# Wider tiles and a re-dealt queue: x in pairs of chunks, N=512 projections, one gate pass and 8 KB weight slots

## The chip, the cores and the metric

One core of a Trainium2 chip runs the kernel. The metric is device time in microseconds (us), the median of several executions; lower is better. A "span" is the time from the first to the last instruction in one profiled execution; here the time is 1.7 to 1.9 us longer than the span. Engines: PE is the matmul engine (PEld its weight loads), DVE the vector engine, ACT the scalar engine, POOL and SP issue transfers. The program fixes the order of each engine's queue, and an entry waits for those ahead of it (in e9 below, the silu, moved behind a scan, starts on DVE at 202.91 instead of 193.59 us).

A run is called slow here only when it lies over 1.5% above the fastest run of the same kernel; where that matters the text says so.

## The reference, cut to what matters

```python
g = sigmoid((x * gate_w).sum(-1))                # gate per token; x is 2048 x 1024, bf16
# A: diagonal state-space layer over the 2048 tokens
Bu = x @ B_bar.T                                 # complex, 1024 states       ("S1")
h[t] = Lam_bar * h[t-1] + Bu[t]                  # recurrence over time       (scans)
a = 2 * Re(h @ C.T) + x * Dskip                  #                            ("S2")
# B: the 8 tokens with the largest x @ w_r go through an expert
idx = argsort(-(x @ w_r))[:8];  xs = x[idx]
y = (silu(xs @ w_gate) * (xs @ w_up)) @ w_down   # weights 1024 x 3584, and 3584 x 1024
b = x + scatter(idx, y * sigmoid(r[idx]))
out = g * a + (1 - g) * b
```

## The kernel before

Time is cut into 8 chunks of 256 tokens. For each chunk PE computes S1, ACT evicts it into V, DVE rotates V (three products, `dve_m`, called "m"), scans it (`dve_scan`) and rotates back (`dve_post`) into H, and PE computes S2 from H. PE also runs the gate pass, the selection of 8 tokens ("sel_a" to "sel_d", with DVE steps in between) and the expert: gate and up products, silu on DVE (`silu_b`), 7 transposes of it (`silu_t`), and the down product `y`.

The order on each engine is fixed by hand: `at(position, f)` queues `f` after the PE work at that position, and entries that fall due together go out in order of their number.

```python
# S1, 256 columns per matmul; [cut]
for dc in range(KD):
    nc.tensor.matmul(vps[:, pl, c, :], lhsT=BT[pl][:, dc, ct * P:(ct + 1) * P], rhs=xT[k][:, dc, :], start=(dc == 0), stop=(dc == KD - 1))
nc.scalar.copy(out=V[k][:, :, 2 * cp:2 * cp + 2, :], in_=vp.pop((k, cp))[:])      # 1024 columns per eviction

# gate pass: x is the stationary side, 2 columns move; 128 matmuls in all; [cut]
nc.tensor.matmul(zc[:, j, :], lhsT=xT[k][:, dc, tl * P:(tl + 1) * P], rhs=rg[:, dc, :], ...)

# order, [cut]
at((2, 7.1), lambda: (dve_post(1, 0, 8), gq.pop("r")(), sel_a2()))      # ahead of m of chunk 2
at((3, 4.1), sel_b2)                                                    # ahead of the scan of chunk 2
at((6, 6.1), silu_a)
at((6, 6.3), silu_b)
# ... the scan of chunk 6 stands at (6, 6.5): behind silu_b
at((7, 1.5), silu_t)
d_pos = [(7, 4)] * 7 + [(8, 4)] * 7                                     # down weights, 512 KB each, freed one by one
```

## Time and profile before

| | before |
|---|---|
| time | 252.34 us (252.07 to 253.46, 4 runs) |
| span | 250.8 us |
| PE / DVE / ACT busy | 244.3 / 232.9 / 101.6 us |
| mean granted clock of PE | 0.999 |

From the page of the kernel before: busy time of each engine; PE's busy share and its granted clock, both in tenths, in 40 slices of the span; the chain that ended last, by engine; and the two large matmul groups (count, then busy us and mean ns of one, then idle time ahead of them).

```profile
PE 244.3 (97%) x1986; PEld 164.2 (65%) x1986; DVE 232.9 (93%) x230; ACT 101.6 (41%) x143; POOL 41.3 (16%) x58
...
PE   8799999999999999999999999999999999999994
...
PEclk9999999999999999999999999999999999999999
...
PE 49%; DVE 41%; SPq 3%; DMA 3%; issue 2%; ACT 0%; DVEq 0%
...
L253 PE MATMUL vps<-xT,BT 128*128 128x256 bf16 x1024 | 114.2, 273 | 1.6 <-DMA BT<-in_A_B_re_dram 0.8
...
L716 PE MATMUL zps<-CT,H 128*128 128x512 bf16 x480 | 105.8, 379 | 0.0
```

The mean of 273 and 379 ns is latency, since matmuls overlap. The pace is read from the chain of waits (start, us, what), where consecutive matmuls are merged:

```profile
15.59 24.63 PE vps L253 x224
...
55.39 10.36 PE zps L716 x48
```

24.63 us for 224 matmuls is 110 ns each at 256 columns; 10.36 us for 48 is 216 ns each at 512. PE runs at that pace from 15.6 to 247.5 us without a gap over 0.5 us. DVE idles for 2.45 us at 84 us and is otherwise full until its last H at 240.9 us, when the last S2 tile has just begun. Both engines are full. From the time lines of PE and of DVE (start, us, engine, line, instruction, count):

```profile
187.42 7.15 PE L253 MATMUL vps<-xT,BT 128*128 128x256 bf16 x64
194.92 0.56 PE L662 MATMUL aT_ps<-ident,gr 128*128 128x128 bf16 x7 [0.35 <-DVE gr L657]
195.32 7.15 PE L253 MATMUL vps<-xT,BT 128*128 128x256 bf16 x64
```

```profile
193.59 0.62 DVE L656 TENSOR_TENSOR sl_e<-gr,sl_e 128x896 bf16<-128x896 bf16 x1
194.24 0.62 DVE L657 TENSOR_TENSOR gr<-sl_e,gr 128x896 bf16<-128x896 bf16 x1
194.78 8.73 DVE L288 TENSOR_TENSOR_SCAN U<-d,U 128x2048 bf16<-128x2048 f32 x2
```

The silu (`gr`) comes just ahead of a 8.7 us pair of scans, and PE waits 0.35 us for it.

### The profile page before, as it was taken

What the parts mean: (1) busy time and instruction counts of PE and PEld (TensorE: products, weight loads), DVE (VectorE), ACT (ScalarE), POOL (GpSimd) and SP (SyncE); (2) the same over time, 40 slices, a digit from 0 to 9 for tenths busy, and PEclk for the clock granted to TensorE, in tenths of its full rate; (3) what the DMA queues carried; (4) which work ended last, traced back from release to release, by engine and by line L of the source; (5) the groups of instructions that cost most, each with busy time, mean ns of one, the idle gap of its engine ahead of it and who ended that gap; (6) DMA issues with size and microseconds to landing.
All of it is one profiled execution on the core that took longest, in us unless ns stands there. A gap on an engine that the chain in (4) does not pass through costs nothing.

```text
span 250.8 us, 4677 instructions
## 1 busy us (share of the span) xinstructions
PE 244.3 (97%) x1986; PEld 164.2 (65%) x1986; DVE 232.9 (93%) x230; ACT 101.6 (41%) x143; POOL 41.3 (16%) x58
## 2 busy tenths in 40 slices
PE   8799999999999999999999999999999999999994
PEld 5688889884678447874487644876448864454453
DVE  1899999999999599999999999999999999999992
ACT  3679981535212322535121372131732335264411
POOL 4020000000000067201400240013101400141520
PEclk9999999999999999999999999999999999999999
DMA  7999999999900202819795587869999829966072
GB/s 182 228 158 238 179 258 211 251 260 261 312 0 3 73 0 89 167 31 348 156 358 190 203 232 236 277 216 338 262 288 293 183 46 277 302 169 178 3 167 84
DMA packets 63492, 48.31 MB, mean 193 GB/s; under 512 B 49504, under 2 KB 51168, under 8 KB 63472
## 3 DMA queue, kind: packets, MB, share of 16 engines
q1 hardware_dynamic: 59056, 37.23, 56.6%
q0 software_dynamic: 4224, 10.53, 17.5%
q8 instruction: 15, 0.25, 0.4%
q10 hardware_dynamic: 192, 0.27, 0.3%
q14 instruction: 5, 0.04, 0.1%
HBM read 27.55 MB, written 8.40 MB: 143 GB/s over the span
## 4 chain that ended last, share of the span: by engine, by line
PE 49%; DVE 41%; SPq 3%; DMA 3%; issue 2%; ACT 0%; DVEq 0%
PE vps L253 22%; PE zps L716 21%; DVE U L288 14%; DVE U L277 4%; DVE U L279 4%; DVE V L278 4%; DVE U L313 4%; DVE H L315 4%; DVE H L311 4%; DVE xt L691 3%; PE zl L730 3%; DMA xT<-in_A_x_dram 3%; SPq L89 2%; PE y L647 1%; PE zc L468 1%
## 5 line engine op out<-in xcount | busy, mean ns | idle before, releaser
L253 PE MATMUL vps<-xT,BT 128*128 128x256 bf16 x1024 | 114.2, 273 | 1.6 <-DMA BT<-in_A_B_re_dram 0.8
L253 PEld LDWEIGHTS <-BT 128*128 128x128 bf16 x1024 | 99.4, 98 | 15.6 <-issue 1.8
L716 PE MATMUL zps<-CT,H 128*128 128x512 bf16 x480 | 105.8, 379 | 0.0
L716 PEld LDWEIGHTS <-H 128*128 128x128 bf16 x480 | 46.3, 98 | 55.7 <-issue 1.9
L288 DVE TENSOR_TENSOR_SCAN U<-d,U 128x2048 bf16<-128x2048 f32 (+1 forms) x20 | 61.7, 3128 | 0.4
L258 ACT CAST V<-vps 128x1024 bf16<-128x1024 f32 x32 | 32.3, 1009 | 60.9 <-PE vps L253 60.9
L719 ACT ACTIVATE ot<-zps,gcol 128x512 bf16<-128x512 f32 x30 | 20.6, 688 | 67.8 <-PE zps L716 65.0
L693 POOL DMA_DIRECT2D out_dram<-xt x14 | 7.8, 561 | 93.1 <-DVE xt L691 92.6
L687 ACT ACTIVATE e<-Dbc,omgcol,gcol 128x1024 f32<-128x1024 bf16 x16 | 18.9, 1233 | 0.0
L691 DVE TENSOR_TENSOR xt<-xt,e 128x1024 bf16<-128x1024 bf16 x16 | 18.8, 1218 | 0.0
L278 DVE TENSOR_TENSOR V<-V,nTi 128x4096 bf16<-128x4096 bf16 (+1 forms) x10 | 16.5, 1652 | 0.5
L277 DVE TENSOR_TENSOR U<-V,T2tab 128x4096 bf16<-128x4096 bf16 (+1 forms) x10 | 16.5, 1645 | 0.5
L279 DVE TENSOR_TENSOR U<-U,V 128x4096 bf16<-128x4096 bf16 (+1 forms) x10 | 16.5, 1652 | 0.3
L554 POOL DMA_INDIRECT xsel<-in_A_x_dram,idx_c x1 | 6.4, 6387 | 61.3 <-ACT ot L719 61.3
L313 DVE TENSOR_TENSOR U<-U,S2tab 128x4096 bf16<-128x4096 bf16 (+1 forms) x8 | 16.2, 2025 | 0.3
L315 DVE TENSOR_TENSOR H<-H,U 128x4096 bf16<-128x4096 bf16 (+1 forms) x8 | 16.2, 2025 | 0.3
L311 DVE TENSOR_TENSOR H<-U,Ctab 128x4096 bf16<-128x4096 bf16 (+1 forms) x8 | 16.1, 2018 | 0.0
L740 POOL DMA_DIRECT2D out_dram<-ot x14 | 14.3, 1048 | 2.0 <-DMA out_dram<-yc,idx_c 2.0
L682 POOL DMA_DIRECT2D xt<-in_A_x_dram x12 | 8.2, 684 | 13.6 <-DMA out_dram<-xt 13.6
L346 DVE TENSOR_TENSOR_SCAN U<-D,U 128x1024 bf16<-128x1024 f32 x4 | 8.9, 2278 | 0.0
L635 PE MATMUL pgu<-wgu,xsel 128*32 128x448 bf16 x128 | 7.4, 355 | 0.0
L730 PE MATMUL zl<-CT,H 128*128 128x256 bf16 (+1 forms) x48 | 7.1, 308 | 0.0
(145 smaller groups left out, 127.9 us busy)
## 6 DMA issues: line engine op xcount, KB each, us to landing
wgu<-in_B_w_gate_dram SPq DMA_DIRECT2D x16, 448.0 KB, 6.4
wgu<-in_B_w_up_dram SPq DMA_DIRECT2D x16, 448.0 KB, 5.7
wd<-in_B_w_down_dram SPq DMA_DIRECT2D x12, 512.0 KB, 6.7
out_dram<-xt POOLq DMA_DIRECT2D x14, 256.0 KB, 2.8
...
```

The lines of the kernel that those rows point to most:

```text
L253: nc.tensor.matmul(vps[:, pl, c, :], lhsT=BT[pl][:, dc, ct * P:(ct + 1) * P], rhs=xT[k][:, dc, :], start=(dc == 0), stop=(dc == KD - 1))
L258: nc.scalar.copy(out=V[k][:, :, 2 * cp:2 * cp + 2, :], in_=vp.pop((k, cp))[:])
L277: nc.vector.tensor_tensor(out=u, in0=v, in1=T2tab[:, :, c0:c1, :], op=ALU.mult)
L278: nc.vector.tensor_tensor(out=v, in0=v, in1=bc(nTi, c0, c1), op=ALU.mult)
L279: nc.vector.tensor_tensor(out=u, in0=u, in1=V[k][:, ::-1, c0:c1, :], op=ALU.add)
L288: nc.vector.tensor_tensor_scan(out=fl, data0=d0[:, c0:c1, :].rearrange("p c t -> p (c t)"), data1=fl, initial=0.0, op0=ALU.mult, op1=ALU.add)
L311: nc.vector.tensor_tensor(out=h, in0=g, in1=bc(Ctab, c0, c1), op=ALU.mult)
L313: nc.vector.tensor_tensor(out=g, in0=g, in1=S2tab[:, :, c0:c1, :], op=ALU.mult)
L315: nc.vector.tensor_tensor(out=h, in0=h, in1=G[k][:, ::-1, c0:c1, :], op=ALU.add)
L691: nc.vector.tensor_tensor(out=xt[:], in0=xt[:], in1=es.pop(b)[:], op=ALU.mult)
L716: nc.tensor.matmul(zps[:], lhsT=H[k][:, pl, ct, tl * P:(tl + 1) * P], rhs=CT[pl][:, ct, dsl], start=(ct == 0 and pl == 0), stop=(ct == NCT ...
L719: nc.scalar.activation(out=ots[b][:, dsl], in_=zps[:], func=ACT.Copy, scale=gcol[:, b:b + 1])
```

## The change

The intent is less PE time: an N=512 matmul reads each weight tile once for two chunks, and a column-tiled gate pass (four weight tiles of 32 columns side by side in PE's array) needs 32 matmuls in place of 128. Chunk x tiles become pairs (`X[m]`), so S1 alternates with S2 in larger blocks: S1 of chunks 2 and 3; S2 of 0 and 1; S1 of 4 and 5; S2 of 2 and 3; S1 of 6 and 7; S2 of 4 to 7. Expert weights are loaded two to a slot of 8 KB per partition, which the x pairs release. All of this needed a new order of queues.

```diff
+    def s1u(m, ct, pl, k0, k1):                       # one weight tile, 512 columns of two chunks
+        o = vp[m, ct][:, pl, k0:k1, :].rearrange("p k t -> p (k t)")
+        ... nc.tensor.matmul(o, lhsT=BT[pl][:, dc, ct * P:(ct + 1) * P], rhs=X[m][:, dc, k0 * LC:k1 * LC], ...)
+    def s1e(m, ct):                                   # two evictions of 512 columns, one for each chunk
+        ... nc.scalar.copy(out=V[k][:, :, ct, :], in_=vp[m, ct][:, :, kk, :])
-    ... zc[:, j, :], lhsT=xT[k][:, dc, tl * P:(tl + 1) * P], rhs=rg[:, dc, :]
+    ... zr[32 * m:32 * m + 32, :], lhsT=rg[:, dc, :], rhs=X[m][:, dc, :]        # 4 column tiles, then 4 transposes
+    def moe_slot(s):
+        for i in range(2):
+            moe_item(2 * s + i, wq[s][0][:, i])
+        free_w.append(wq.pop(s)[1])                   # a slot is released after both its weights are used
+        load_w()
[... cut ...]
+    at((1, 1.5), lambda: dve_m(2, 0, 8))
+    at((1, 1.6), sel_a2)                              # now behind m of chunk 2
+    at((1, 3.9), sel_b)
+    at((2, 1.5), lambda: dve_scan(2, 0, 8))
+    at((2, 2.0), sel_b2)                              # now behind the scan of chunk 2
[... cut ...]
+    at((7, 1.95), silu_a)
+    at((7, 1.96), silu_b)
+    at((7, 3.9), silu_t)
+    at((7, 0.5), lambda: dve_m(6, 0, 8))
+    at((7, 1.5), lambda: dve_scan(6, 0, 8))           # now ahead of silu_b
[... cut ...]
+    pos = [(3, 2.9)] * 2 + ... + [(7, 1.9)] * 2 + [(8, 0.9)] * 4 + [(8, 3.9)] * 3      # the last 7 slots are down weights
+    blocks = [(1, None), (None, 0), (None, 1), (2, None), (None, 2), (None, 3), (3, None)] + [(None, k) for k in range(4, NK)]
```

More of the change, by code (lines that the diff above doesn't have):

```diff
@@ L69, with load_B @@
     ps_m = ctx.enter_context(tc.tile_pool(name="ps_m", bufs=2, space=PSUM))
-    xT = [const.tile([P, KD, LC], BF16, name=f"xT{k}", tag=f"xT{k}") for k in range(5)]
+    X = {}
     BT = [const.tile([P, KD, NP_], BF16, name=f"BT{pl}") for pl in range(2)]
     CT = [const.tile([P, NCT, D], BF16, name=f"CT{pl}") for pl in range(2)]
-    x0r = const.tile([P, BPC, D], BF16, name="x0r", tag="xT5")
+    x0r = const.tile([P, BPC, D], BF16, name="x0r", tag="XP2")
     for tl in range(BPC):
         nc.sync.dma_start(x0r[:, tl, :], x2d[tl * P:(tl + 1) * P, :])
+    def load_B(pl, c0, c1):
+        nc.sync.dma_start_transpose(BT[pl][:, :, c0 * P:c1 * P], Bsrc[pl][c0 * P:c1 * P, :])
+    for pl in range(2):
+        load_B(pl, 0, 2)
     vrow = small.tile([NCT, 5, P], BF16, name="vrow", tag="va")
@@ L80, with new_X, load_X @@
         nc.scalar.dma_start(vrow[:, i, :], v.rearrange("(c p) -> c p", p=P))
+    def new_X(m):
+        X[m] = const.tile([P, KD, 2 * LC], BF16, name=f"X{m}", tag=f"XP{m}")
     def load_xT(k):
-        if k >= len(xT):
-            xT.append(const.tile([P, KD, LC], BF16, name=f"xT{k}", tag=f"xT{k}"))
-        nc.sync.dma_start_transpose(xT[k][:], x2d[k * LC:(k + 1) * LC, :])
-    def load_B(c0, c1):
-        for pl in range(2):
-            nc.sync.dma_start_transpose(BT[pl][:, :, c0 * P:c1 * P], Bsrc[pl][c0 * P:c1 * P, :])
-    load_B(0, 2)
-    load_xT(1)
-    load_xT(2)
-    for c0 in range(2, NCT, 2):
-        load_B(c0, c0 + 2)
+        m, kk = divmod(k, 2)
+        nc.sync.dma_start_transpose(X[m][:, :, kk * LC:(kk + 1) * LC], x2d[k * LC:(k + 1) * LC, :])
+    def load_X(m):
+        new_X(m)
+        load_xT(2 * m)
+        load_xT(2 * m + 1)
+    new_X(0)
+    load_xT(1)
+    for c0 in range(2, NCT, 2):
+        for pl in range(2):
+            load_B(pl, c0, c0 + 2)
+    load_X(1)
     for d0_ in range(0, D, 512):
@@ L127 @@
     M = {}
+    rg = small.tile([P, KD, 32], BF16, name="rg")
+    nc.gpsimd.memset(rg[:], 0.0)
     ones16 = small.tile([NTT, 8], BF16, name="ones16")
@@ L144 @@
             nc.tensor.transpose(xq[:, dc, :], x0r[:, tl, dc * P:(dc + 1) * P], ident[:])
-        (nc.scalar.copy if tl == 0 else nc.vector.tensor_copy)(out=xT[0][:, :, tl * P:(tl + 1) * P], in_=xq[:])
+        (nc.scalar.copy if tl == 0 else nc.vector.tensor_copy)(out=X[0][:, :, tl * P:(tl + 1) * P], in_=xq[:])
         if tl == 0:
@@ L187, in tab_arg @@
     def tab_arg(q):
-        u = const.tile([P, QC, LC], F32, name="tu", tag="xT7")
+        ur = const.tile([P, 2, QC, LC], F32, name="tu", tag="XP3")
+        u, rn = ur[:, 0], ur[:, 1]
         for c in range(QC):
@@ L191, in tab_arg @@
             nc.vector.tensor_scalar(out=u[:, c, :], in0=ramp[:], scalar1=thp[:, ct:ct + 1], scalar2=None, op0=ALU.mult)
-        rn = const.tile([P, QC, LC], F32, name="trn", tag="xT6")
-        nc.vector.tensor_scalar(out=rn[:], in0=u[:], scalar1=MAGIC, scalar2=MAGIC, op0=ALU.add, op1=ALU.subtract)
+        nc.vector.tensor_scalar(out=rn, in0=u, scalar1=MAGIC, scalar2=MAGIC, op0=ALU.add, op1=ALU.subtract)
         f = tabp.tile([P, QC, LC], F32, name="tf", tag="tf", bufs=2)
-        nc.vector.tensor_tensor(out=f[:], in0=u[:], in1=rn[:], op=ALU.subtract)
+        nc.vector.tensor_tensor(out=f[:], in0=u, in1=rn, op=ALU.subtract)
         tabs[q] = [f]
@@ L214, in tab_bwd_s @@
         f, af = tabs.pop(q)
-        S32 = (tabp, const)[q].tile([P, QC, LC], F32, name="tS", tag=("ta", "xT7")[q])
-        nc.scalar.activation(out=S32[:], in_=f[:], func=ACT.Sin, scale=TWO_PI)
-        C32 = (tabp, const)[q].tile([P, QC, LC], F32, name="tC", tag=("tb", "xT6")[q])
-        nc.scalar.activation(out=C32[:], in_=af[:], func=ACT.Sin, scale=-TWO_PI, bias=halfpi[:])
+        if q:
+            S32, C32 = (sc[:, i] for sc in [const.tile([P, 2, QC, LC], F32, name="tSC", tag="XP3")] for i in range(2))
+        else:
+            S32, C32 = (tabp.tile([P, QC, LC], F32, name=n, tag=t)[:] for n, t in (("tS", "ta"), ("tC", "tb")))
+        nc.scalar.activation(out=S32, in_=f[:], func=ACT.Sin, scale=TWO_PI)
+        nc.scalar.activation(out=C32, in_=af[:], func=ACT.Sin, scale=-TWO_PI, bias=halfpi[:])
         tabs[q] = (S32, C32)
@@ L223, in tab_bwd_q @@
             S32, C32 = tabs.pop(q)
-            q1 = (tabp, const)[q].tile([P, QC, LC], F32, name="tq", tag=("tq", "xT5")[q])
+            q1 = tabp.tile([P, QC, LC], F32, name="tq", tag="tq")
         else:
@@ L245, with s1x, s1 @@
     vp = {}
-    def s1u(k, cp, c, pl):
-        if (k, cp) not in vp:
-            vp[k, cp] = ps_s1.tile([P, 2, 2, LC], F32, name="vps", tag="vps")
-        vps = vp[k, cp]
-        ct = 2 * cp + c
-        for dc in range(KD):
-            nc.tensor.matmul(vps[:, pl, c, :], lhsT=BT[pl][:, dc, ct * P:(ct + 1) * P], rhs=xT[k][:, dc, :], start=(dc == 0), stop=(dc == KD - 1))
-    def s1e(k, cp):
-        if k not in V:
-            V[k] = big_new("V", k)
-        nc.scalar.copy(out=V[k][:, :, 2 * cp:2 * cp + 2, :], in_=vp.pop((k, cp))[:])
-    def s1(k, cp):
+    def s1u(m, ct, pl, k0, k1):
+        if (m, ct) not in vp:
+            vp[m, ct] = ps_s1.tile([P, 2, 2, LC], F32, name="vps", tag="vps")
+        o = vp[m, ct][:, pl, k0:k1, :].rearrange("p k t -> p (k t)")
+        for dc in range(KD):
+            nc.tensor.matmul(o, lhsT=BT[pl][:, dc, ct * P:(ct + 1) * P], rhs=X[m][:, dc, k0 * LC:k1 * LC], start=(dc == 0), stop=(dc == KD - 1))
+    def s1e(m, ct):
+        for kk in range(2):
+            k = 2 * m + kk
+            if k not in V:
+                V[k] = big_new("V", k)
+            nc.scalar.copy(out=V[k][:, :, ct, :], in_=vp[m, ct][:, :, kk, :])
+        vp.pop((m, ct))
+    def s1x(k, cp):
+        vps = ps_s1.tile([P, 2, 2, LC], F32, name="vps", tag="vps")
         for pl in range(2):
             for c in range(2):
-                s1u(k, cp, c, pl)
-        s1e(k, cp)
+                ct = 2 * cp + c
+                for dc in range(KD):
+                    nc.tensor.matmul(vps[:, pl, c, :], lhsT=BT[pl][:, dc, ct * P:(ct + 1) * P], rhs=X[0][:, dc, k * LC:(k + 1) * LC], start=(dc == 0), stop=(dc == KD - 1))
+        V[k] = big_new("V", k)
+        nc.scalar.copy(out=V[k][:, :, 2 * cp:2 * cp + 2, :], in_=vps[:])
+    def s1(m, ct):
+        for pl in range(2):
+            s1u(m, ct, pl, 0, 2)
+        s1e(m, ct)
     G = {}
@@ L378 @@
     warm(7)
-    for pl in range(2):
-        for c in range(2):
-            s1u(0, 0, c, pl)
-    s1e(0, 0)
+    s1x(0, 0)
     d0_cp(0, 2)
+    tab_bwd_s(0)
     sq = sm("sq", [P, 2, NCT])
@@ L410 @@
     nc.vector.tensor_scalar(out=rs4[:, 1, 0, :], in0=rot[:, 1, 1, :], scalar1=-1.0, scalar2=None, op0=ALU.mult)
-    s1(1, 0)
-    d0_cp(2, 4)
+    s1x(1, 0)
     tab_arg(1)
     tab_abs(1)
-    tab_bwd_s(0)
-    dve_m(0, 0, 2)
-    dve_scan0(0, 0, 2)
     vb_ps = ps_m.tile([P, 2, NCT], BF16, name="vb_ps", tag="m")
@@ L421 @@
         nc.tensor.transpose(vb_ps[:, i, :], vrow[:, 3 + i, :], ident[:NCT, :NCT])
-    rg = small.tile([P, KD, 2], BF16, name="rg")
-    nc.vector.tensor_copy(rg[:].rearrange("p k t -> p t k"), vb_ps[:])
+    nc.vector.tensor_copy(rg[:, :, 0:2].rearrange("p k t -> p t k"), vb_ps[:])
     gwc = rg[:, :, 1:2]
+    dve_m(0, 0, 2)
+    dve_scan0(0, 0, 2)
     tab_bwd_q(0, 0, 2)
-    s1(2, 0)
+    s1(0, 2)
+    d0_cp(2, 4)
     tab_bwd_q(0, 2, 4)
+    s1(0, 3)
     tab_bwd_b(0)
-    s1(0, 1)
     dve_m(0, 2, 4)
@@ L433 @@
     tab_fwd(1)
-    s1(1, 1)
     tab_neg(1)
-    d0_cp(4, 8)
+    s1(0, 4)
+    d0_cp(4, 6)
     tab_bwd_s(1)
-    s1(0, 2)
-    tab_bwd_q(1, 0, 2)
-    dve_post(0, 0, 4)
-    s1(2, 1)
-    tab_bwd_q(1, 2, 4)
+    s1(0, 5)
     dve_m(0, 4, 6)
     dve_scan0(0, 4, 6)
-    s1(0, 3)
+    d0_cp(6, 8)
+    tab_bwd_q(1, 0, 1)
+    s1(0, 6)
+    tab_bwd_q(1, 1, 3)
+    s1(0, 7)
+    tab_bwd_q(1, 3, 4)
     dve_m(0, 6, 8)
@@ L448 @@
     dve_state(0, 4, 8)
-    s1(1, 2)
     tab_bwd_b(1)
+    dve_post(0, 0, 8)
     def sigm(pool, z_ap, shape, tagp):
-        e = pool.tile(shape, BF16, name=tagp + "_e")
+        e = pool.tile(shape, BF16, name=tagp + "_e", tag={"sl": "mg"}.get(tagp, tagp))
         nc.scalar.activation(out=e[:], in_=z_ap, func=ACT.Sigmoid)
@@ L459, with gate_rows @@
     omgcol = small.tile([P, NTT], F32, name="omgcol")
-    def gate_cols(k0, k1):
-        n = (k1 - k0) * BPC
-        zc = ps_m.tile([P, n, 2], F32, name="zc", tag="m")
-        for k in range(k0, k1):
-            for tl in range(BPC):
-                j = (k - k0) * BPC + tl
-                for dc in range(KD):
-                    nc.tensor.matmul(zc[:, j, :], lhsT=xT[k][:, dc, tl * P:(tl + 1) * P], rhs=rg[:, dc, :], start=(dc == 0), stop=(dc == KD - 1))
-        sl = slice(k0 * BPC, k1 * BPC)
-        zb = small.tile([P, n], BF16, name=f"zb{k0}")
-        nc.scalar.copy(out=zb[:], in_=zc[:, :, 1])
-        nc.scalar.copy(out=rcb[:, sl], in_=zc[:, :, 0])
-        ex = sigm(small, zb[:], [P, n], f"gc{k0}")
-        def rest():
-            gb = ex
-            nc.vector.tensor_copy(gcol[:, sl], gb[:])
-            ob = small.tile([P, n], BF16, name=f"ob{k0}")
-            nc.vector.tensor_scalar(out=ob[:], in0=gb[:], scalar1=-1.0, scalar2=1.0, op0=ALU.mult, op1=ALU.add)
-            nc.vector.tensor_copy(omgcol[:, sl], ob[:])
-        return rest
+    def gate_rows():
+        zr = ps_m.tile([P, 2 * LC], F32, name="zr", tag="m")
+        for dc in range(KD):
+            for m in range(4):
+                nc.tensor.matmul(zr[32 * m:32 * m + 32, :], lhsT=rg[:, dc, :], rhs=X[m][:, dc, :], start=(dc == 0), stop=(dc == KD - 1), skip_group_check=True)
+        M["zrb"] = small.tile([P, 2 * LC], BF16, name="zrb", tag="va")
+        nc.scalar.copy(out=M["zrb"][:], in_=zr[:])
@@ new lines, in gate_cols @@
+    def gate_cols():
+        zt = ps_m.tile([P, 4, P], BF16, name="zt", tag="m")
+        for tq in range(4):
+            nc.tensor.transpose(zt[:, tq, :], M["zrb"][:, tq * P:(tq + 1) * P], ident[:])
+        zv = zt[:].rearrange("p t (j s) -> p j t s", s=32)
+        zb = small.tile([P, NTT], BF16, name="zb")
+        nc.scalar.copy(out=zb[:].rearrange("p (j t) -> p j t", t=4), in_=zv[:, :, :, 1])
+        gb = sigm(small, zb[:], [P, NTT], "gc")
+        nc.scalar.copy(out=gcol[:], in_=gb[:])
+        nc.scalar.copy(out=rcb[:].rearrange("p (j t) -> p j t", t=4), in_=zv[:, :, :, 0])
+        ob = small.tile([P, NTT], BF16, name="ob")
+        nc.scalar.activation(out=ob[:], in_=gb[:], func=ACT.Copy, scale=-1.0, bias=1.0)
+        nc.scalar.copy(out=omgcol[:], in_=ob[:])
+        M["aT"] = small.tile([P, NFC // 4, 4, 32], BF16, name="aT", tag="va")
+        nc.gpsimd.memset(M["aT"][:], 0.0)
@@ L485 @@
     nc.gpsimd.memset(M["xsel32"][:], 0.0)
-    M["aT"] = small.tile([P, NFC // 4, 4, 32], BF16, name="aT", tag="va")
-    nc.gpsimd.memset(M["aT"][:], 0.0)
-    g0 = gate_cols(0, 3)
-    s1(1, 3)
-    g0()
-    dve_post(0, 4, 8)
     pro.close()
@@ L600 @@
     NW = NGU + NFP
+    NS = NW // 2
     wq = {}
@@ L605, in load_w, with moe_item @@
     def load_w():
-        while nload[0] < NW and free_w:
-            i = nload[0]
-            pool, tag = free_w.pop(0)
-            if i < NGU:
-                h, r = divmod(i, 2 * KD)
-                dc, k = divmod(r, 2)
-                w = pool.tile([P, NG, FH], BF16, name="wgu", tag=tag)
-                nc.sync.dma_start(w[:], (wg_v, wu_v)[k][:, dc, h])
-            else:
-                jp, c = divmod(i - NGU, NFB)
-                w = pool.tile([P, 2, D], BF16, name="wd", tag=tag)
-                p0 = 0
-                while p0 < P:
-                    h, o = divmod(c * P + p0, FH)
-                    n = min(P - p0, FH - o)
-                    nc.sync.dma_start(w[p0:p0 + n], wd_v[o:o + n, h, 2 * jp:2 * jp + 2, :])
-                    p0 += n
-            wq[i] = (w, pool, tag)
-            nload[0] += 1
-    def moe_item(i):
-        w, pool, tag = wq.pop(i)
+        while nload[0] < NS and free_w:
+            s = nload[0]
+            tag = free_w.pop(0)
+            if s < NGU // 2:
+                h, dc = divmod(s, KD)
+                w = const.tile([P, 2, NG, FH], BF16, name="wgu", tag=tag)
+                for k in range(2):
+                    nc.sync.dma_start(w[:, k], (wg_v, wu_v)[k][:, dc, h])
+            else:
+                w = const.tile([P, 2, 2, D], BF16, name="wd", tag=tag)
+                for i in range(2):
+                    jp, c = divmod(2 * (s - NGU // 2) + i, NFB)
+                    p0 = 0
+                    while p0 < P:
+                        h, o = divmod(c * P + p0, FH)
+                        n = min(P - p0, FH - o)
+                        nc.sync.dma_start(w[p0:p0 + n, i], wd_v[o:o + n, h, 2 * jp:2 * jp + 2, :])
+                        p0 += n
+            wq[s] = (w, tag)
+            nload[0] += 1
+    def moe_slot(s):
+        for i in range(2):
+            moe_item(2 * s + i, wq[s][0][:, i])
+        free_w.append(wq.pop(s)[1])
+        load_w()
+    def moe_item(i, w):
         if i < NGU:
@@ L647, in moe_item @@
                     nc.tensor.matmul(y4[32 * g:32 * g + 32, :], lhsT=aT[:, c, 2 * jp + ji, :], rhs=w[:, ji, g * DG:(g + 1) * DG], start=(i == NGU and ji == 0), stop=(i == NW - 1 and ji == 1), skip_group_check=True)
-        free_w.append((pool, tag))
-        load_w()
     def silu_a():
@@ L700, in scatter_upd @@
         nc.gpsimd.indirect_dma_start(out=out2d[:, :], out_offset=bass.IndirectOffsetOnAxis(ap=M["idx_c"][:, :1], axis=0), in_=M["upd"][:], in_offset=None, bounds_check=L - 1, oob_is_err=False, compute_op=ALU.add)
-        pool, tag = free_w.pop(0)
-        M["ul"] = pool.tile([P, BPC, D], BF16, name="ul", tag=tag)
+        M["ul"] = const.tile([P, BPC, D], BF16, name="ul", tag=free_w.pop(0))
         nc.sync.dma_start(M["ul"][:], out2d[TLAST:, :].rearrange("(r p) d -> p r d", p=P))
@@ L760, in at @@
         pending.append((pos, len(pending), fn))
-    load_xT(3)
-    load_xT(4)
+    load_X(2)
+    load_X(3)
     for b in range(4):
         load_x(b)
-    for k in range(5, NK):
-        load_xT(k)
-    s1(2, 2)
-    s1(2, 3)
-    s1(3, 0)
-    dve_m(1, 0, 8)
-    dve_scan(1, 0, 8)
-    gq = {}
-    at((2, 6), lambda: gq.update(r=gate_cols(3, 8)))
-    at((2, 7), sel_a)
-    at((2, 7.1), lambda: (dve_post(1, 0, 8), gq.pop("r")(), sel_a2()))
-    at((3, 4), sel_b)
-    at((3, 4.1), sel_b2)
-    at((4, 2), sel_c)
@@ L781 @@
-    at((4, 3), sel_d)
-    at((4, 5.4), lambda: (sel_c2(), sel_d2()))
-    at((3, 4), load_w)
-    gu_pos = [(4, 3)] * 4 + [(4, 6)] * 4 + [(5, 1)] * 4 + [(5, 4)] * 4 + [(5, 7)] * 5 + [(6, 2)] * 5 + [(6, 5)] * 6
-    for i in range(NGU):
-        at(gu_pos[i], lambda i=i: moe_item(i))
-    at((6, 6.1), silu_a)
-    at((6, 6.3), silu_b)
-    at((7, 1.5), silu_t)
-    d_pos = [(7, 4)] * 7 + [(8, 4)] * 7
-    for i in range(NFP):
-        at(d_pos[i], lambda i=i: moe_item(NGU + i))
-    at((8, 4.15), fin_a)
@@ L794 @@
-    at((8, 4.17), lambda: (fin_b(), scatter_upd()))
-    for k in range(2, NK):
-        late = k == 2
-        if k == NK - 1:
-            at((k, 4.5), lambda: last_m(0))
-        else:
-            at((3, 1.3) if late else (k, 4.5), lambda k=k: dve_m(k, 0, 8))
-        at((3, 4.2) if late else (4, 0.6) if k == 3 else (k, 4.6), lambda k=k: rows(k - 1))
-        if k > 3:
-            at((k, 4.1), lambda k=k: rows_e(k - 1))
-        if k == NK - 1:
-            at((k, 5.5), lambda: last_scan(0))
-            at((k, 4.2), d0_short)
-            at((k, 7.2), lambda: last_post(0, 0, NCT))
-        else:
-            at((3, 4.3) if late else (4, 0.7) if k == 3 else (k, 6.5) if k == 6 else (k, 5.5), lambda k=k: dve_scan(k, 0, 8))
-            at((3, 4.4) if late else (4, 0.8) if k == 3 else (k, 7.2), lambda k=k: dve_post(k, 0, 8))
-        for i in range(2):
-            at((3, 4.25) if late else (4, 0.65) if k == 3 else (k, 5.9 + 2 * i), lambda b=2 * k - 4 + i: fin(b))
@@ L814, with m_scan @@
-    at((2, 4.4), lambda: rows_e(1))
-    at((4, 0.5), lambda: rows_e(2))
-    at((NK, 4.1), lambda: (rows_e(NK - 1), rows(NK - 1)))
-    at((NK, 4.2), lambda: last_m(1))
-    at((NK, 4.3), lambda: last_scan(1))
-    at((NK, 4.35), lambda: (last_post(1, 0, NCT // 2), last_post(1, NCT // 2, NCT)))
-    at((NK, 6.5), lambda: (rows_e(NK), rows(NK), add_upd(NTT - 2), add_upd(NTT - 1)))
-    for i in range(2):
-        at((NK, 5.9 + 2 * i), lambda b=NTT - 4 + i: fin(b))
-    at((3, 1.5), zero_last)
+    def m_scan(k):
+        dve_m(k, 0, 8)
+        dve_scan(k, 0, 8)
@@ new lines @@
+    at((0, 4.5), lambda: m_scan(1))
+    at((0, 6.5), gate_rows)
+    at((0, 7.5), gate_cols)
+    at((1, 0.5), lambda: dve_post(1, 0, 8))
+    at((1, 0.9), sel_a)
+    at((1, 1.5), lambda: dve_m(2, 0, 8))
+    at((1, 1.6), sel_a2)
+    at((1, 3.9), sel_b)
+    at((2, 0.0), zero_last)
+    at((2, 1.5), lambda: dve_scan(2, 0, 8))
+    at((2, 2.0), sel_b2)
+    at((2, 3.5), lambda: dve_post(2, 0, 8))
+    at((2, 3.6), lambda: (rows_e(1), rows(1), fin(0), fin(1)))
+    at((3, 0.9), sel_c)
+    at((3, 1.5), lambda: dve_m(3, 0, 8))
@@ new lines @@
+    at((3, 2.2), lambda: (rows_e(2), rows(2), fin(2), fin(3)))
+    at((3, 2.8), sel_d)
+    at((3, 4.5), lambda: (dve_scan(3, 0, 8), sel_c2(), sel_d2()))
+    at((3, 6.5), lambda: dve_post(3, 0, 8))
+    at((4, 0.5), lambda: dve_m(4, 0, 8))
+    at((4, 1.5), lambda: dve_scan(4, 0, 8))
+    at((4, 3.6), lambda: (rows(3), fin(4), fin(5)))
+    at((5, 0.5), lambda: dve_post(4, 0, 8))
+    at((5, 0.6), lambda: (rows_e(4), rows(4)))
+    at((5, 2.5), lambda: fin(6))
+    at((5, 3.9), lambda: fin(7))
@@ new lines @@
+    at((5, 2.6), lambda: dve_m(5, 0, 8))
+    at((6, 1.0), lambda: dve_scan(5, 0, 8))
+    at((4, 2.2), lambda: rows_e(3))
+    at((6, 1.2), lambda: (rows_e(5), rows(5)))
+    at((6, 4.0), lambda: dve_post(5, 0, 8))
+    at((6, 5.2), lambda: (rows_e(6), rows(6)))
+    at((7, 1.95), silu_a)
[3 more added lines that the diff above has]
+    at((7, 1.5), lambda: dve_scan(6, 0, 8))
+    at((7, 2.5), lambda: fin(8))
+    at((7, 3.9), lambda: fin(9))
@@ new lines @@
+    at((7, 3.5), lambda: dve_post(6, 0, 8))
+    at((7, 2.2), lambda: rows_e(7))
+    at((8, 0.5), d0_short)
+    at((8, 0.6), lambda: rows(7))
+    at((8, 1.0), lambda: last_m(0))
+    at((8, 2.0), lambda: last_scan(0))
+    at((8, 2.5), lambda: fin(10))
+    at((8, 3.95), lambda: fin(11))
+    at((8, 3.92), fin_a)
+    at((8, 3.94), lambda: (fin_b(), scatter_upd()))
+    at((9, 0.0), lambda: last_m(1))
+    at((9, 0.1), lambda: last_post(0, 0, NCT))
+    at((9, 0.5), lambda: last_scan(1))
+    at((9, 2.5), lambda: fin(12))
@@ L825 @@
+    at((9, 3.9), lambda: fin(13))
+    at((9, 3.0), lambda: (last_post(1, 0, NCT // 2), last_post(1, NCT // 2, NCT)))
+    at((10, 0.5), lambda: (rows_e(NK), rows(NK), add_upd(NTT - 2), add_upd(NTT - 1)))
+    pos = [(3, 2.9)] * 2 + [(4, 1.9)] * 3 + [(5, 1.9)] * 3 + [(6, 1.9)] * 3 + [(6, 5.9)] * 3 + [(7, 1.9)] * 2 + [(8, 0.9)] * 4 + [(8, 3.9)] * 3
+    for s in range(NW // 2):
+        at(pos[s], lambda s=s: moe_slot(s))
     pending.sort(key=lambda e: (e[0], e[1]))
@@ L829, in run @@
             pending.pop(0)[2]()
-    for n in range(2, NK + 2):
-        if n >= 3:
-            if n == 3:
-                free_w.extend((const, f"xT{i}") for i in range(3))
-            elif n <= NK:
-                free_w.append((const, f"xT{n - 1}"))
-            if n >= 4:
-                load_w()
-        for cp in range(4):
-            if 2 < n < NK and (n, cp) != (3, 0):
-                s1(n, cp)
-            run((n, cp + 0.99))
-        for i, b in enumerate((2 * (n - 2), 2 * (n - 2) + 1)):
+    blocks = [(1, None), (None, 0), (None, 1), (2, None), (None, 2), (None, 3), (3, None)] + [(None, k) for k in range(4, NK)]
+    fill = {1: ("XP0", "XP1"), 4: ("XP2",), 7: ("XP3",)}
+    for n, (m, k) in enumerate(blocks):
+        free_w.extend(fill.get(n, ()))
+        load_w()
+        if k is None:
+            for ct in range(NCT):
+                s1(m, ct)
+                run((n, ct + 0.99))
+            continue
+        for i, b in enumerate((2 * k, 2 * k + 1)):
             if b == NTT - 1:
@@ L848 @@
                 s2(b, dh)
-                run((n, 4 + 2 * i + dh + 0.99))
+                run((n, 2 * i + dh + 0.99))
                 if b == NTT - 2 and dh == 1:
```

## The prediction

> **What bounds it now.** The clock was full (0.999). The page gives PE 244.3 and DVE 232.9 of 250.8 us busy. PE's time line has no gap over 0.5 us from 15.6 to 247.5 us, and S1 runs at 110 ns per N=256 matmul (224 in 24.63 us in the chain of waits), S2 at 216 ns per N=512 (48 in 10.36): PE runs at pace. The busy column, 273 and 379 ns, is overlapped time, as the Trainium skill warns (Trainium Kernel Development and Optimization, opening note: matmul busy time is a bad metric because matmuls are pipelined). DVE idles before its first work, 2.45 us at 84 us (selection waiting for PE), and after its last H at 240.9 us; the last S2 tile starts at 240.5 us. One DVE chunk costs 25.4 us (products 7.0, row products 2.3, scans 8.8, post 7.0). DVE has no slack.
>
> **Removed.** 896 of 1024 N=256 S1 matmuls become 448 at N=512: 896 x 110 - 448 x 216 ns = 1.8 us. The gate's 128 matmuls took 3.2 us (chain: 1.18 + 1.98); 32 column-tiled ones are estimated at 1.8 us plus 0.3 of transposes, from the expert pass, where 56 column-tiled N=256 took 1.64 us (the skill agrees: TensorE: Matmul & The Clock Gate, Part 3, column tiles run concurrently). PE saves about 3 us. DVE saves 0.8 us of gate columns, 0.4 of split posts, and its 2.45 us wait.
>
> **Added.** ACT evicts each S1 pair as two 512-column copies, estimated 2 x 0.6 us against 0.9 (the 512-column ot eviction took 0.69 with latency): 9 us more, harmless except in the prologue, where ACT is 99% busy at 20 to 30 us: about 2 us of DVE wait.
>
> **Moved**, which matters most; I added trace durations along the three queues in the new order.
> - idx_c comes after scan 2 on DVE, near 96 us; xsel landed 8.7 us after idx_c in the trace; PE reaches the xsel transposes near 102 us and waits about 3 us (was none). PE also waits 3 us for the first selection product.
> - S1 for chunks 6 and 7 therefore ends near 192 us, and DVE waits about 4 us for V of chunk 6.
> - silu_b now stands behind scan 6 and one more pair of row products on DVE, and ends near 206 to 210 us (was 194.9). PE still has silu_t, three S2 chunks and the down pass after it, 45 us, and waits 3 us at silu_t. Even without new DVE waits silu_b would end near 202.3, the whole near 248 (was 247.5): no net gain possible.
> - The second batch of down weights, 3.1 MB, has 11 us between its slots' release and its use (before: 15.5 us for 3.7 MB); at that stage's 248 to 298 GB/s it is 0 to 2 us late.
>
> All lie on the PE/DVE chain. Sum: the last S2 ends near 256 instead of 247.5 us.
>
> **Prediction.** 259 us, 8 in 10 between 252 and 264.5. Faster by over 2%: 0.04; within 2%: 0.34; slower: 0.62.
>
> **What would show it.** S1 near 216 ns per matmul and a gate pass near 1.8 us; PE waits at the xsel transposes, at silu_t (released by DVE gr), perhaps at the down pass (DMA wd); a DVE wait for V of chunk 6; ACT busy near 110 us. Span minus PE waits should be about 248.
>
> **What would make it wrong.** DVE 5 us ahead of my sums (ACT not holding it in the prologue) makes a tie; an N=512 pass below 216 ns would give a gain; late transposed x for the gate pass (all of x is needed near 61 us, estimated landing 61 to 62) or late weights would add loss.

## The result, and the profile after

Ratios here and below are the mean time of one kernel's fast runs over that of the other's of the same rounds, so not quite the ratio of the medians.

| | before | after |
|---|---|---|
| time | 252.34 us | 265.32 us (263.72 to 267.22, 4 runs) |
| ratio to before | | 1.0509 (95% interval 1.0432 to 1.0585) |
| span | 250.8 us | 263.3 us |
| PE / DVE / ACT busy | 244.3 / 232.9 / 101.6 us | 245.7 / 232.6 / 104.5 us |
| mean granted clock of PE | 0.999 | 0.981 |

The page of the kernel after, the same lines:

```profile
PE 245.7 (93%) x1390; PEld 116.6 (44%) x1414; DVE 232.6 (88%) x221; ACT 104.5 (40%) x174; POOL 35.4 (13%) x60
...
PE   8799999999993999999999999999999499889994
...
PEclk9999999999998699999999999999999979999999
...
PE 61%; DVE 24%; DMA 7%; SPq 5%; issue 1%; ACT 0%; DVEq 0%
...
L738 PE MATMUL zps<-CT,H 128*128 128x512 bf16 x470 | 108.8, 389 | 0.6 <-issue 0.2
L266 PE MATMUL vps<-X,BT 128*128 128x512 bf16 x467 | 104.3, 379 | 0.9 <-DMA BT<-in_A_B_im_dram 0.3
```

Two dents stand in PE's row, and each is followed by a dent in the clock row. (Some matmul records are missing from this trace, which is why the counts are 470 and 467 instead of 480.) PE's time line shows what happens there; in brackets, the idle time ahead of an instruction and what ended it:

```profile
70.17 10.53 PE L738 MATMUL zps<-CT,H 128*128 128x512 bf16 x47
84.67 0.36 PE L542 MATMUL fl_ps<-mm,ones 16*8 16x128 bf16 x2 [3.97 <-DVE mm L534]
84.97 16.75 PE L738 MATMUL zps<-CT,H 128*128 128x512 bf16 x63
101.55 3.62 PE L266 MATMUL vps<-X,BT 128*128 128x512 bf16 x15
105.10 0.35 PE L579 MATMUL xselT_ps<-ident,xsel 8*128 8x8 bf16 x8
...
199.48 7.08 PE L738 MATMUL zps<-CT,H 128*128 128x512 bf16 x31
210.18 0.93 PE L685 MATMUL aT_ps<-ident,gr 128*128 128x128 bf16 x7 [3.62 <-DVE gr L680]
210.90 4.89 PE L738 MATMUL zps<-CT,H 128*128 128x512 bf16 x15
215.72 1.93 PE L672 MATMUL y<-wd,aT 128*32 128x256 bf16 x64
...
228.05 1.06 PE L672 MATMUL y<-wd,aT 128*32 128x256 bf16 x32
230.54 0.40 PE L672 MATMUL y<-wd,aT 128*32 128x256 bf16 x8 [1.43 <-DMA wd<-in_B_w_down_dram]
231.84 0.40 PE L672 MATMUL y<-wd,aT 128*32 128x256 bf16 x8 [0.90 <-DMA wd<-in_B_w_down_dram]
232.17 20.89 PE L738 MATMUL zps<-CT,H 128*128 128x512 bf16 x94
```

PE waits three times: 3.97 us for the first selection product, 3.62 us for the silu, 2.33 us for down weights. The first two waits cost twice. The S2 chunk after the first took 16.6 us (84.97 to 101.55) where an S2 chunk takes 13.8; the S2 tile after the second took 4.8 us where 3.5 is normal, and the 7 transposes 0.93 where the kernel before needed 0.56. Stretches of the same trace show why (window, its length, busy us and counts of each engine, then the mean granted clock, the DMA share and GB/s):

```profile
83.80:90.63 6.83, 5.96 (x16) 2.15 (x17) 6.79 (x7) 0.36 (x1) 0.00 (x0) 0.50 0.00 0
91.40:101.50 10.10, 10.05 (x47) 4.61 (x47) 9.69 (x18) 2.06 (x3) 2.05 (x1) 1.00 0.02 3
210.09:213.51 3.42, 3.33 (x14) 1.68 (x15) 3.38 (x3) 0.35 (x1) 0.00 (x0) 0.51 0.26 49
217.90:228.00 10.10, 10.10 (x47) 4.42 (x46) 9.79 (x9) 1.37 (x2) 2.02 (x3) 1.00 1.03 293
```

The granted clock was halved, for 6.8 us at the first wait (from 83.8 us on, 0.9 us before the wait ended) and for 3.4 us at the second; then it is 1.00 again. Once PE has work in these windows it reads as "busy", with 16 matmuls in 5.96 us of it. Only the count and the clock show the loss.

DVE's time line shows why the silu is late:

```profile
186.80 2.35 DVE L714 TENSOR_TENSOR xt<-xt,e 128x1024 bf16<-128x1024 bf16 x2
192.42 2.29 DVE L302 TENSOR_TENSOR U<-V,T2tab 128x4096 bf16<-128x4096 bf16 x1 [3.27 <-ACT V L273]
...
199.73 8.74 DVE L313 TENSOR_TENSOR_SCAN U<-d,U 128x2048 bf16<-128x2048 f32 x2
...
208.84 0.62 DVE L679 TENSOR_TENSOR sl_e<-gr,sl_e 128x896 bf16<-128x896 bf16 x1
209.50 0.62 DVE L680 TENSOR_TENSOR gr<-sl_e,gr 128x896 bf16<-128x896 bf16 x1
```

DVE waits for V of chunk 6, multiplies, scans for 8.7 us, and only then makes the silu, though PE had finished the gate and up products by 199.5 us. PE meanwhile stands at the transposes. The next S2 tile, whose H DVE had finished by 186.9 us, is queued behind them; placing the transposes later on PE, instead of the silu earlier on DVE, was not tried.

**An account of PE's time.** The last S2 ended at 247.45 us before and at 260.01 us after, 12.6 us later. PE work saved, from the paces measured: S1 896 x 110 ns less 448 x 216 ns is 1.8 us, the gate pass 1.1 us (below). Lost: waits of 3.97 and 3.62 us; slow matmuls after them, 2.8 us (16.6 for 13.8) and 1.7 us (4.8 for 3.5, and 0.93 for 0.56); the second down pass 2.7 us (4.12 us from 228.05 to 232.17, where the same pass took 1.43 in a later run). The sum is 14.8 - 2.9 = 11.9 us of the 12.6.

### The profile page after: what moved, and what is told of

Its sections match the earlier page's. It is cut to its first block, busy times and chain, and to the rows that moved or that the text cites. A ratio compares the mean times of both kernels' runs of the same rounds, so it can differ in the third digit from the quotient of the medians.

```text
span 263.3 us, 3515 instructions
## 1 busy us (share of the span) xinstructions
PE 245.7 (93%) x1390; PEld 116.6 (44%) x1414; DVE 232.6 (88%) x221; ACT 104.5 (40%) x174; POOL 35.4 (13%) x60
## 4 chain that ended last, share of the span: by engine, by line
PE 61%; DVE 24%; DMA 7%; SPq 5%; issue 1%; ACT 0%; DVEq 0%
PE vps L266 28%; PE zps L738 26%; DVE U L313 8%; DMA wd<-in_B_w_down_dram 5%; DVE U L302 3%; DVE U L304 3%; DVE V L303 3%; SPq L80 3%; PE zl L752 3%; DMA BT<-in_A_B_im_dram 2%; PE pgu L660 2%; DVE H L340 2%; DVE U L338 2%; DVE H L336 2%; PE y L672 1%
## 5 line engine op out<-in xcount | busy, mean ns | idle before, releaser
L738 PE MATMUL zps<-CT,H 128*128 128x512 bf16 x470 | 108.8, 389 | 0.6 <-issue 0.2
L266 PE MATMUL vps<-X,BT 128*128 128x512 bf16 x467 | 104.3, 379 | 0.9 <-DMA BT<-in_A_B_im_dram 0.3
L738 PEld LDWEIGHTS <-H 128*128 128x128 bf16 x480 | 47.4, 100 | 59.4 <-issue 7.0
L266 PEld LDWEIGHTS <-BT 128*128 128x128 bf16 x480 | 46.4, 98 | 57.2 <-DMA BT<-in_A_B_im_dram 0.8
L273 ACT CAST V<-vps 128x512 bf16<-128x512 f32 x60 | 32.2, 588 | 55.0 <-PE vps L266 52.6
L338 DVE TENSOR_TENSOR U<-U,S2tab 128x4096 bf16<-128x4096 bf16 x7 | 16.0, 2292 | 0.2
L340 DVE TENSOR_TENSOR H<-H,U 128x4096 bf16<-128x4096 bf16 x7 | 16.0, 2292 | 0.2
L336 DVE TENSOR_TENSOR H<-U,Ctab 128x4096 bf16<-128x4096 bf16 x7 | 16.0, 2281 | 0.0
L282 PE MATMUL vps<-X,BT 128*128 128x256 bf16 x64 | 7.5, 273 | 1.4 <-DMA BT<-in_A_B_re_dram 0.8
L282 PEld LDWEIGHTS <-BT 128*128 128x128 bf16 x64 | 6.1, 98 | 2.8 <-DMA BT<-in_A_B_re_dram 1.1
```

The lines of the kernel that those rows point to most:

```text
L266: nc.tensor.matmul(o, lhsT=BT[pl][:, dc, ct * P:(ct + 1) * P], rhs=X[m][:, dc, k0 * LC:k1 * LC], start=(dc == 0), stop=(dc == KD - 1))
L273: nc.scalar.copy(out=V[k][:, :, ct, :], in_=vp[m, ct][:, :, kk, :])
L336: nc.vector.tensor_tensor(out=h, in0=g, in1=bc(Ctab, c0, c1), op=ALU.mult)
L338: nc.vector.tensor_tensor(out=g, in0=g, in1=S2tab[:, :, c0:c1, :], op=ALU.mult)
L340: nc.vector.tensor_tensor(out=h, in0=h, in1=G[k][:, ::-1, c0:c1, :], op=ALU.add)
L738: nc.tensor.matmul(zps[:], lhsT=H[k][:, pl, ct, tl * P:(tl + 1) * P], rhs=CT[pl][:, ct, dsl], start=(ct == 0 and pl == 0), stop=(ct == NCT ...
```

## The experiments

Three theories stood at the outset. *Order*: the new order of the DVE queue makes PE wait, and an idle PE then loses clock; late weights are a smaller term. *Grain*: pairs of 512 columns cost time whatever the order. *Weights*: the 8 KB slots deliver late and set the pace of the whole. Results at a glance; each ratio is to the kernel before in its own rounds. The medians are over all runs, slow ones included (one in e2 and e3, two in e4); the ratios are over fast runs alone.

| run | edit | median us | ratio to before (95%) |
|---|---|---|---|
| after | the change | 265.32 | 1.0509 (1.0432 to 1.0585) |
| e1_silu_first | silu ahead of scan 6 | 258.68 | 1.0189 (1.0132 to 1.0247) |
| e2_select_first | selection steps earlier | 261.24 | 1.0306 (1.0221 to 1.0391) |
| e3_both_first | e1 and e2 | 252.97 | 0.9988 (0.9954 to 1.0022) |
| e4_pe_filled | after, with PE's wait filled | 267.35 | 1.0460 (1.0384 to 1.0535) |
| e8_only_weights | after, with weights requested sooner | 263.29 | 1.0416 (1.0377 to 1.0455) |
| e9_before_silu_late | before, with silu behind scan 6 | 263.90 | 1.0430 (1.0404 to 1.0456) |
| e5_weights_sooner | e3, with weights requested sooner | 251.15 | 0.9930 (0.9897 to 0.9963) |
| e6_s1_at_256 | e5, with S1 at 256 columns | 252.19 | 0.9997 (0.9964 to 1.0029) |
| e7_gate_as_before | e5, with the old gate pass | 251.66 | 0.9967 (0.9926 to 1.0009) |

All nine experiments gave correct results.

### e1_silu_first

```diff
-    at((7, 1.5), lambda: dve_scan(6, 0, 8))
+    at((7, 1.97), lambda: dve_scan(6, 0, 8))
```

> Edit: scan of chunk 6 is queued on DVE behind silu_b instead of ahead of it, nothing else. Order theory (the new order of the DVE queue makes PE wait, and an idle PE then loses clock): the 3.6 us wait of PE at the silu transposes goes, and so does the slow S2 tile after it (4.9 us where 3.5 is normal): about 260.5 us, 4 to 5 below the changed kernel. DVE will wait about 2 us for the silu instead, off the critical path. Weight theory (the 8 KB slots deliver late and set the pace): the wait moves to the down pass, time stays within 1 us of 265. Grain theory (pairs of 512 columns cost whatever the order): 264 to 266.

Measured: 258.68 us, 6.6 us below the changed kernel and 1.8 better than expected. PE's time line:

```profile
197.30 7.08 PE L738 MATMUL zps<-CT,H 128*128 128x512 bf16 x31
204.22 0.55 PE L685 MATMUL aT_ps<-ident,gr 128*128 128x128 bf16 x7
204.61 3.62 PE L738 MATMUL zps<-CT,H 128*128 128x512 bf16 x15
```

The wait is gone and the tile after it is normal. DVE waits 1.6 us for the silu's input instead. PE does not feel it: H of chunk 6 is done at 216.3 us, and PE takes it at 224.3. One line of order, with pairs and slots unchanged, moved half of the loss, which neither rival allows. The extra 1.8 us has a likely reason in this trace: PE still waited for the selection product, 3.37 us, but the next S2 chunk ran at a clock of 1.00 and took 13.8 us. So a wait of 3.4 us need not cost clock, while those of 3.6 and 4.0 us did. Length alone does not decide it, however. In the same trace PE waited only 1.82 us (221.97 to 223.79) for down weights, among column-tiled matmuls, and the clock was then 0.50 from 224.2 to 227.3 us. Why is not known.

### e2_select_first

```diff
-    at((1, 1.6), sel_a2)
+    at((1, 1.4), sel_a2)
-    at((2, 2.0), sel_b2)
+    at((2, 1.4), sel_b2)
```

> Edit: both selection steps on DVE stand ahead of the products of chunk 2 and of scan 2, instead of behind them; nothing else. Order theory: PE's 4.0 us wait for the first selection product goes, S2 of chunk 1 runs at 216 ns per matmul again (266 in the changed kernel, after that wait), xsel is there when PE needs it, DVE's 3.3 us wait for V of chunk 6 falls to about 1; the wait at the silu transposes stays: about 260.5 us. Weight theory and grain theory: 264 to 266.

Measured: 261.24 us, against 260.5 expected. PE did not wait for the selection, S2 of chunk 1 took 13.8 us, and DVE did not wait for V of chunk 6 (3.3 us after). The silu wait stayed, 3.98 us, with a slow tile of 4.9 us behind it.

### e3_both_first

The edit is both of the above.

> Edit: both of the reorderings of the two runs before. Order theory: their sum, 255 to 257 us, with PE waiting only at the down pass, and the granted clock back at 0.99 or more. Weight theory and grain theory: 263 to 266.

Measured: 252.97 us, the same as before (ratio 0.9988), 2 to 4 us better than expected. The clock is 0.998 to 1.000 in its four fast runs. Two reorderings, of one and of two queue entries, take back the whole 13 us. The fifth run, 256.71 us at a clock of 0.984, is a slow one, and it is the one with a profile: in it PE waited 3.3 us for down weights and the clock was 0.50 for 6.8 us from 219.6 us on. In the fast runs the clock was not lost; what PE waited for weights there is not known.

### e4_pe_filled

```diff
+    def pefill(n):
+        w = ps_m.tile([P, LC], F32, name="wfill", tag="m")
+        for _ in range(n):
+            nc.tensor.matmul(w[:], lhsT=BT[0][:, 0, 0:P], rhs=BT[0][:, 0, 0:LC], start=True, stop=True)
-    at((7, 3.9), silu_t)
+    at((7, 3.9), lambda: (pefill(34), silu_t()))
```

> Edit: the changed kernel, with 34 idle matmuls of 256 columns (about 3.7 us) put on PE just ahead of the silu transposes, where it waits 3.6 us. If idling costs clock: no clock drop after the silu transposes, the next S2 tile takes 3.5 instead of 4.8 us, and the time falls by about 1.4 us to 264 although PE has more work. If the lower clock has another cause: the S2 tile stays at 4.8 us and the time stays at 265 or rises a little.

Measured: 267.35 us over all four runs; the mean of its two fast runs is 264.9 (ratio 1.0460 against 1.0509). The time is inconclusive: the expected 1.4 us is inside the spread of 263.6 to 268.6 us. The profiled run is a slow one, but the place in question can be read by itself:

```profile
207.31 3.87 PE L782 MATMUL wfill<-BT 128*128 128x256 bf16 x34
211.09 0.56 PE L685 MATMUL aT_ps<-ident,gr 128*128 128x128 bf16 x7
211.49 3.62 PE L738 MATMUL zps<-CT,H 128*128 128x512 bf16 x15
```

With PE kept at work, the transposes took 0.56 us and the S2 tile 3.5, at full clock. In the three traces in which the same wait stood unfilled (after, e2 and e8: 3.6 to 4.0 us) the transposes took 0.90 to 0.93 us and the next work was slow. So it is the idling that costs the clock there, as far as one filled trace against three can show it. The gain did not reach the end of this run: PE arrived at the down pass and waited 4.35 us for weights (2.33 after), with a lower clock after that.

### e8_only_weights

```diff
-    pos = ... + [(8, 0.9)] * 4 + ...
+    pos = ... + [(7, 3.95)] * 2 + [(8, 0.9)] * 2 + ...
```

> Edit, on the changed kernel itself with its own order: two of the four first down-weight slots are used right behind the silu transposes. Order theory with late weights as one term of the sum: PE's waits for down weights (2.3 us) shrink to under 1 us and the time falls by 1.5 to 2.5 us to about 263; the waits for the selection and the silu stay. Weight theory (the slots set the pace of the whole): it falls by more than 5 us.

Measured: 263.29 us, 2.0 us less, as the order theory had it; the two intervals overlap a little, so the size is rough. The waits for down weights are gone from the trace (the second batch runs from 228.83 to 230.26 us, 1.43 us); the waits for the selection (3.96) and for the silu (3.62) stay. Late weights are a term of about 2 us, not the pace of the kernel. The same 3.62 us wait was followed here by a clock of 0.50 for 6.8 us (208.6 to 215.4), twice as long as in the changed kernel. Whether the lateness of the weights comes from the 8 KB slots or from where the slots were put in the order was not separated.

### e9_before_silu_late

The opposite test: the one bad queue position, put into the old kernel.

```diff
-    at((6, 6.3), silu_b)
+    at((6, 6.6), silu_b)
```

> Edit, on the kernel before: silu on DVE is queued behind the scan of chunk 6 (it stood ahead of it), nothing else; chunks, slots and gate stay as before. Order theory: silu ends 8.8 us later, near 203.7 us instead of 194.9; PE, which is at the silu transposes at 194.5, waits about 9 us and has slow matmuls after it: 261 to 264 us, so the order alone does to the old kernel most of what the change did. Grain theory and weight theory (the pairs or the 8 KB slots are what cost): 252 to 254 us, DVE's queue having room.

Measured: 263.90 us against 252.98, in the expected range. PE's time line, to be held against the three lines of the kernel before:

```profile
188.44 7.15 PE L253 MATMUL vps<-xT,BT 128*128 128x256 bf16 x64
204.24 0.93 PE L662 MATMUL aT_ps<-ident,gr 128*128 128x128 bf16 x7 [8.65 <-DVE gr L657]
204.96 9.54 PE L253 MATMUL vps<-xT,BT 128*128 128x256 bf16 x64
```

The wait is 8.65 us, and 64 matmuls that took 7.15 us take 9.54 after it. No pair, no 8 KB slot and no wide matmul is in this kernel. This settles that the order of DVE's queue suffices for a loss of this size.

### e5_weights_sooner

On top of e3:

```diff
-    at((7, 3.9), silu_t)
+    at((7, 2.9), silu_t)
-    pos = ... + [(8, 0.9)] * 4 + ...
+    pos = ... + [(7, 3.9)] * 2 + [(8, 0.9)] * 2 + ...
```

> Edit, on top of both reorderings: the silu transposes come one S2 tile earlier, and two of the four first down-weight slots are used one S2 tile earlier, so their slots are released and refilled about 4 us sooner. Estimate from the trace of both_first: PE's 3.3 us of waits for down weights go, and the lower clock after them: 249 to 250 us, about 1.2% below the kernel before. If the weights are not what holds PE there (rival: S2 of chunk 6 waits for DVE in any case), the time stays at 253.

Measured: 251.15 us, ratio 0.9930 (0.9897 to 0.9963). It beats both kernels, though by 0.7% and not by the 1.2% hoped for. The clock is 0.999 or 1.000 in all six runs. The down pass no longer waits:

```profile
197.37 0.55 PE L685 MATMUL aT_ps<-ident,gr 128*128 128x128 bf16 x7
...
201.30 1.06 PE L672 MATMUL y<-wd,aT 128*32 128x256 bf16 x32
...
205.85 1.06 PE L672 MATMUL y<-wd,aT 128*32 128x256 bf16 x32
...
217.30 1.49 PE L672 MATMUL y<-wd,aT 128*32 128x256 bf16 x48
```

What is left between the saving of 2.9 us and the 0.9 us by which the last S2 ends earlier (246.6 against 247.45 us) is partly visible: 0.6 us of waiting for the second B tile at 17 us and 0.7 us for an eviction by ACT at 151.5 us.

### e6_s1_at_256

On top of e5, S1 runs as two passes of 256 columns:

```diff
-        o = vp[m, ct][:, pl, k0:k1, :].rearrange("p k t -> p (k t)")
-        for dc in range(KD):
-            nc.tensor.matmul(o, ... rhs=X[m][:, dc, k0 * LC:k1 * LC], ...)
+        for k in range(k0, k1):
+            for dc in range(KD):
+                nc.tensor.matmul(vp[m, ct][:, pl, k, :], ... rhs=X[m][:, dc, k * LC:(k + 1) * LC], ...)
```

> Edit, on top of weights_sooner: S1 of the pairs runs as two passes of 256 columns for each weight plane again, everything else kept. The width alone: 448 matmuls of 512 at 216 ns become 896 at 110 ns, PE work rises by 1.8 us, of which most is on the critical chain of PE: 1.0 to 1.8 us slower than weights_sooner. If the width gives more than that (weight loads no longer hidden, say), the difference is 3 us or more.

Measured: 252.19 us; the quotient of the two ratios (0.9997 / 0.9930) is 1.0067, so 1.7 us slower than e5, inside the expectation. The two intervals only just part, so the size is rough, and the two profiled executions do not show it (spans of 249.9 us in e5 and 249.5 in e6). The width of 512 is worth a little, perhaps 1 to 2 us.

### e7_gate_as_before

On top of e5, 128 matmuls with x as the stationary side, as before (the diff is cut; the 4 transposes go too):

```diff
-                nc.tensor.matmul(zr[32 * m:32 * m + 32, :], lhsT=rg[:, dc, :], rhs=X[m][:, dc, :], ...)
+                nc.tensor.matmul(zc[:, j, :], lhsT=X[m][:, dc, tq * P:(tq + 1) * P], rhs=rg[:, dc, 0:2], ...)
```

> Edit, on top of weights_sooner: the gate pass with x as the stationary side, 128 matmuls of 2 columns as before, in place of 32 column-tiled matmuls and 4 transposes. PE work rises by 3.2 - 2.2 = 1.0 us: 0 to 1 us slower than weights_sooner, the time unchanged if PE has slack at that place (DVE still has the products of chunk 1 in hand there).

Measured: 251.66 us, 0.9 us slower than e5 by the ratios, inside the expectation, but the intervals overlap, so it is not shown apart from zero. The trace of e7 held something not expected. Stretches of it, during the pass and after it:

```profile
60.30:63.40 3.10, 3.10 (x128) 3.10 (x127) 3.10 (x1) 1.07 (x2) 0.00 (x0) 1.00 0.82 261
63.50:68.50 5.00, 4.95 (x18) 1.88 (x16) 5.00 (x2) 0.00 (x0) 0.00 (x0) 0.66 0.39 135
```

PE was never idle, yet after 3.1 us of matmuls with 2 columns the mean clock was 0.66 for 5 us (0.50 from 64.5 to 67.5), and the next 16 S1 matmuls took 5.1 us (3.5 is normal). Three of the six e7 runs had a mean clock below 0.995; all six of e5 had 0.999 or more. In the kernel before the pass comes in pieces of 1.2 and 2.0 us, and the clock stayed at 1.00.

## Why the prediction was wrong, point by point

The direction was right, and so were the waits at the selection and the silu. What the mechanism lacked was the clock that PE loses after a wait. The loss was 13.0 us where 6.7 were forecast, and the time lay just above the range.

- **PE work saved.** Right. S1 ran at 216 ns per matmul; the gate pass took 1.84 us (60.94 to 62.78 us in the trace) with 0.23 us of transposes, where 1.8 and 0.3 were forecast.
- **ACT.** Too high: 104.5 us busy, not about 110. DVE waited 0.97 us for an eviction of V in the prologue, where about 2 were forecast.
- **Selection.** "PE also waits 3 us for the first selection product": right in kind, 3.97 us.
- **xsel.** "PE reaches the xsel transposes near 102 us and waits about 3 us": wrong. PE came at 105.10 us and waited for nothing. The slow S2 chunk after the selection wait had made it 2.8 us late, and xsel is sooner than forecast: in e1 PE used it without a wait at 103.14 us, 5.9 us after idx_c, where the forecast had 8.7 us.
- **V of chunk 6.** "DVE waits about 4 us": 3.3 us.
- **silu.** "ends near 206 to 210 us ... waits 3 us at silu_t": right. It ended at 210.1 us, and PE waited 3.62 us.
- **Down weights.** "0 to 2 us late": 2.33 us of waits, 2.7 us with what follows.
- **The check it named.** "Span minus PE waits should be about 248": the span less the three long waits is 263.3 - 3.97 - 3.62 - 2.33 = 253.4 us. This is the clearest sign of what was missing: PE was not only waiting longer, it was also working slower.

The step that failed is the one that turns waits into time: **"All lie on the PE/DVE chain. Sum: the last S2 ends near 256 instead of 247.5 us."** It has three mis-sized terms.

1. *A wait of PE was costed at its own length.* The halved clock costs more: 2.8 us after the first wait and 1.7 us after the second. The first stood where the forecast had a 3 us wait for xsel that did not come, so by luck the two errors nearly cancelled; the second lies at the end, where nothing takes it up. The Trainium skill says this on the very page that the prediction cites (TensorE: Matmul & The Clock Gate, "Why this matters for your kernels": no PE gaps over about 3 us between bursts, or the clock falls to half; the trace shows 0.50), and the forecast had waits of 3 us in it. The page was cited and this row not applied. The traces agree in part: 3.62, 3.97 and 8.65 us of idling were each followed by slow matmuls, 3.37 us were not, but 1.82 us among the down matmuls of e1 were. The same page (Part 1) gives a free-running window of 3.4 us, which would make a wait of about that length a matter of chance; no run here tests that.
2. *The down weights*, 2.7 us where the sum had about 1.
3. *The step from the last S2 to the time.* The prediction added 3 us (256 to 259). In the kernel before it is 252.34 - 247.45 = 4.9 us, which could have been read from its trace and its time. That alone is 2 us.

Of the 6.3 us between 259 and 265.3, items 1 and 2 explain about 3.4 and item 3 about 2. The remaining 0.9 us is not pinned down: the selection and silu waits were 1.0 and 0.6 us longer than the 3 us forecast, the prediction does not itemise its sum, and the runs of the kernel after spread over 3.5 us.

"No net gain possible" needs a limit. It was true of the order given, but not of the change. With the DVE queue and the weights re-dealt, the same pairs, gate pass and slots run at 251.15 us.

Shown by experiment: the order of DVE's queue accounts for the whole net loss of 13 us (e3 takes it back, e9 puts a loss of 11 us into the old kernel). Late weights are about 2 us (e8) of the gross loss, which is larger than the net one by what the change saves. The wide matmuls help at most a little (e6). Not separated: slot size against slot position.

## What to carry to other kernels

When two engines are both full, a change that saves a few microseconds on one of them is decided by the order of the other's queue: put short steps that an engine waits for ahead of long ones that nobody waits for yet. In these traces every wait on PE of 3.6 us or more was followed by 1.7 to 2.8 us of lost time on slow matmuls, so cost such a wait with both. One of 3.37 us was not, and one of 1.82 us in a down pass was: no safe length is shown. Look at the granted clock in the stretch behind a gap, because PE reads as 100% busy there. Before reading the sum, carry the known distance between the last matmul and the reported time over from the kernel at hand.

## What the Trainium skill lacked or had wrong

- *TensorE: Matmul & The Clock Gate* does not say what a short wait costs between column-tiled matmuls: in e1 1.82 us of it were followed by a clock of 0.50 for over 3 us, where 3.37 us between full-width matmuls were followed by 1.00.
- Nor does the page say that a stream of ordinary matmuls with almost no moving columns can lower the clock with PE busy throughout: after 128 matmuls of 2 columns in 3.1 us the mean granted clock was 0.66 for 5 us (e7).
- The same page, "Back-to-back issue gap", gives about 131 ns per N=512 matmul as the sustained pace in a real stream of weight loads and matmuls, below its isolated 216 ns. The chain of the kernel before shows 216 ns at N=512 (10.36 us for 48) and 110 ns at N=256 with a weight load for each matmul; nothing near 131 ns was seen.
- The same page, Part 3, measures three column tiles at 2.38 times and has no figure for four. Four column tiles at N=512 took 1.84 us for 32 matmuls, 57.5 ns each, which is 3.8 times as fast as 216 ns.
